# Masks, memory term and token rows as 64-row matmuls in an attention, mixture-of-experts and MLP kernel

## The chip, the cores and the metric

One core of a Trainium2 chip runs the whole program. The metric is the device time of one execution in microseconds (us).

## The reference, cut to what matters

The kernel computes three stages one after another: attention with a memory term, a mixture of experts with one expert per token, and an MLP. The change is in the first, and in the passage from the first to the second.

```python
# attention: B, H, S, D = 4, 8, 576, 64
scores = scale * np.matmul(q, k.transpose(0, 1, 3, 2))
scores = np.where(causal, -1e9, scores)
a = np.exp(scores - scores.max(-1, keepdims=True))
a /= a.sum(-1, keepdims=True) + 1e-09
local = np.matmul(a, v)
q_p = phi(q)
mem_out = einsum('bhsd,bhde->bhse', q_p, M_prev) / (einsum('bhsd,bhd->bhs', q_p, z_prev)[..., None] + 1e-06)
attn = g * mem_out + (1 - g) * local                  # g = sigmoid(beta), per head
# mixture of experts: N, D, E, F = 2304, 512, 8, 1024
logits = x @ w_gate;  e = argmax(logits);  gate_w = softmax(logits)[e]
out = gate_w * (np.maximum(x @ w1[e], 0.0) @ w2[e])
# MLP: 2304 tokens, 512 -> 2048 -> 512, ELU between
```

All is float32 with an accuracy that a single pass of TensorE in reduced precision does not give, so products are made of two halves (hi and lo) in three passes, or as float32 matmuls, which the trace shows as two instructions each.

## The kernel before, in words

**Attention.** A pair is two heads of one batch; there are 16 pairs (4 batches of 4). The 128 partitions hold two heads of 64 dimensions. The 576 query rows are cut into four row tiles of 128 and a short one of 64. For each pair the function `attention` (its inner function `pair`) records these operations:

- q and k are loaded, transposed on TensorE (L549) and split into halves in the table `ab`; phi(q), transposed, is `qpT`.
- Score tiles. For row tiles 0 to 3, `scores` issues six matmuls (L634): three hi and lo combinations for each of two heads, each contracting over that head's 64 partitions, so that the two heads' matmuls use the upper and the lower half of the array. The causal mask follows as a matmul of the bf16 identity with a mask table (L636), one per head, over all 128 rows. The short row tile holds both heads as the rows of one tile, with six 128-row matmuls (L642) and a mask (L643). A score tile takes a two-bank PSUM tile, one bank per head.
- VectorE takes the row minimum (scores carry a negative sign, L651), ScalarE the exponential with its row sum (L656).
- TensorE transposes the weights block by block (L668); ScalarE or VectorE evacuates each block into `aA` (row tiles 0 to 2) or `aB` (3 and 4) (L504, L507).
- The products with v (L771): each head's result goes to 64 of the 128 output partitions.
- The memory term (L739): per row tile one float32 matmul of `qpT` over 128 rows against the table `mb`, which holds one head's columns for the upper 64 rows and the other's for the lower 64, zeros elsewhere, 146 columns. Token rows (L787): likewise `xT`, the product transposed, against the table `iw` (identity and gate weights, 144 columns). Both are made as two blocks of three and two row tiles, in one-bank tiles.
- VectorE scales both (L755 and L792), POOL adds them into the token rows and logits (L803).
- After the last pair of a batch `gate_plan` makes the routing of the batch (L909, L1021 and others).

**PSUM in this stage** is four one-bank tiles (ring `rw`) and two two-bank tiles (ring `rx`, for score tiles and the transposes of q and k).

**What sets the order.** The operations are not run in the order in which they are recorded. Each is handed to a `Plan` with its engine or engines, a cost in ns, what it reads and writes, and a priority: 1000 per pair plus an offset from the table `KNOBS` (`off`). `Plan.order` is a list scheduler: it keeps a time for each engine, takes those operations whose inputs and buffers are there, and among those that could start within a slack it takes the one of lowest priority number. It decides between ScalarE and VectorE too where both are named. `emit` issues the instructions in that order; after that each engine runs in order.

**The passage.** The attention stage and the expert stage are two plans. In the second the first tile's rows of x (table `ex`, gathered in the first) are transposed (L1223), split into halves (L1185 and L1188, in the helper `split`), weights are split part by part in the same helper (eight parts of 1024 columns), and the first expert matmul follows (L1277). The second product of the experts is L1320. The MLP stage is `moe2`.

Of the kernel before, what the change touches and what calls it, by code (L numbers as in the profile page):

```python
# [79 lines left out]
class Op:  # L80
    __slots__ = ("eng", "cost", "fn", "prio", "lat", "need", "users", "slots", "ready", "start", "seq", "why", "dma", "lag", "waits", "dense", "span")


class Plan:
# [10 lines left out]
    def __init__(self, slack=0.0, begin=(), warm=1.0e4, wait=0.0):  # L95
        self.slack, self.begin, self.warm, self.wait = slack, dict(begin), warm, wait
        self.ops, self.wr, self.rd, self.base = [], {}, {}, 0.0

    def op(self, eng, cost, fn, r=(), w=(), prio=0.0, dma=0.0, lag=0.0, dense=1.0, span=(0.0, 1.0e9)):
        o = Op()  # L100
        o.dense, o.span = dense, span
# [33 lines left out]
    def order(self):  # L135
        ready, free, done, queue, work = {}, {}, [], 0.0, {}
# [6 lines left out]
        while len(done) < len(self.ops):  # L143
            best = None
            for e, lst in ready.items():
                cand = []
                for o in lst:
# [17 lines left out]
                    cand.append((t, o.prio, o.seq, o))  # L165
# [21 lines left out]
            if e == "PE":  # L187
# [3 lines left out]
                end = t + o.cost * (1.0 + cold) + (self.wait if o.waits else 0.0)  # L191
# [32 lines left out]
    "m_g": -500, "wq": 0.85, "sa": 60.0, "sm": 50.0, "s2": 0.0, "step": -140.72, "hd": 3300.14,  # L224
    "mem": 23753.60, "xg": 4,
    "wh": [("ACT", "DVE"), ("ACT", "DVE"), ("ACT", "DVE"), ("DVE",), ("ACT",), ("ACT", "DVE"), ("ACT", "DVE"), ("ACT", "DVE")],
    "wl": [("DVE",)] * 8, "ord": [4, 2, 3, 1, 0], "rings": 2, "ab": 2,
    "busy": [0, 0, 0], "early": -20000.00, "late": 500, "mld": -14323.58, "gate": -27170.79,
    "warm": [52, 0.0, 200.0], "qe": ("DVE",),
    "off": {"tk": -12817.78, "tq": -13488.70, "hi": -2210.28, "lo": -31413.21, "px": 6755.77, "phi": -79534.02, "F": -5913.349368048794, "S": 17790.71, "min": 19452.13, "exp": 27411.30, "T": 14069.74, "Te": -6480.68, "fin": 55325.15, "mm": 81816.08, "md": -23369.51, "ms": 75715.68, "av": 48586.94, "ave": 30515.56, "rw": 59524.12, "ls": -7182.97, "add": 6568.91},  # L230
    "wait": 25
# [19 lines left out]
def constants(tc, ctx, c, M_prev, z_prev, beta, w_gate):  # L251
# [12 lines left out]

    c.swap = c.ap.tile([P, P], F32, name="swap")
# [10 lines left out]
    c.iw = c.ap.tile([P, H // 2, 2 * XB], F32, name="iw")  # L276

    MW = XB + 1
    c.mb = c.ap.tile([P, NPAIR, 2 * MW], F32, name="mb")
# [11 lines left out]
    pl.op("POOL", 2600, f, w=["mb", "iw"], prio=400.0)  # L291

    def f():
        for h in range(2):
            nc.sync.dma_start(c.mb[hss[h], :, h * MW:h * MW + D], Mv[h])
        nc.sync.dma_start(wg, w_gate.rearrange("(h d) e -> d h e", d=D))
        nc.sync.dma_start(zr, z_prev.rearrange("b h d -> (b h) d"))
    pl.op("SP", 2600, f, w=["mld"], prio=K["mld"], dma=3000)

    def f():  # L300
        for h in range(2):
            nc.sync.dma_start(c.iw[hss[h], :, h * XB + D:(h + 1) * XB], wv[h])
# [3 lines left out]
    def f():  # L306
        for h in range(2):
            for hp in range(H // 2):
                nc.vector.tensor_copy(c.iw[hss[h], hp, h * XB:h * XB + D], c.ident[hss[h], hss[h]])
# [12 lines left out]
    for h in range(2):  # L322
        for n in range(2):
            def mk(h, n):
                bk = Slot(c.rs)

                def f():
                    for x in range(8):
                        nc.tensor.transpose(bk.t[0:D, x * D:(x + 1) * D], c.mb[hss[h], 8 * n + x, h * MW:h * MW + D], c.ident[hss[h], hss[h]])
                pl.op("PE", 450, f, r=["mld"], w=[bk], prio=K["mem"] - 30)  # L330

                def f():
                    nc.scalar.copy(mT[:, h, 8 * n:8 * n + 8, :].rearrange("p x d -> p (x d)"), bk.t[0:D, :])
                pl.op("ACT", ca(512), f, r=[bk], w=[("mT", h, n)], prio=K["mem"] - 30)
            mk(h, n)
    for h in range(2):
        def mk(h):
# [8 lines left out]
            def f():  # L346
                nc.vector.tensor_copy(c.mb[hss[h], :, h * MW + D:h * MW + XB], bq.t[hss[h], 0:NPAIR * E].rearrange("p (x e) -> p x e", e=E))
                nc.vector.tensor_copy(c.mb[hss[h], :, h * MW + XB:(h + 1) * MW].rearrange("p x o -> p (x o)"),
# [1370 lines left out]
```

## Time and profile before

| what | us |
|---|---|
| three runs | 1000.88, 1000.12, 998.05 |
| their median | 1000.12 |
| the profiled execution | 999.02 |
| its span in the profile | 996.9 |
| TensorE busy | 963.7 |
| TensorE's weight loads | 789.9 |
| VectorE busy | 651.6 |
| ScalarE busy | 453.1 |
| GpSimd (POOL) busy | 140.2 |

The span is what the profiler saw from the first to the last instruction; the execution's own time is 2.1 us more. Weight loads are a row of their own, since they run beside the matmuls. Attention fills the time to about 270 us, the experts to about 592, the MLP the rest.

### The profile page before, as it was taken

How to read it: one execution, taken by the hardware profiler on the slowest of the kernel's cores; microseconds unless marked ns; L12 is line 12 of the kernel's file. 1: busy time of each engine (PE TensorE's matmuls, PEld its weight loads, DVE VectorE, ACT ScalarE, POOL GpSimd, SP SyncE). 2: the span in 40 equal slices, each digit the busy share in tenths (PEclk: the TensorE clock that was granted, in tenths of full speed). 3: DMA queues.
4: the chain of work that ended last, by engine and by line, in shares of the span. 5: the costliest groups of instructions: out<-in, count | busy, mean ns of one | idle time of the engine just before them, and what ended most of it. 6: DMA issues, size and time to landing. Idle time of an engine off the chain costs nothing. (4 is left out here: it accounts for less than half of the span.)

```text
span 996.9 us, 16392 instructions
## 1 busy us (share of the span) xinstructions
PE 963.7 (97%) x5770; PEld 789.9 (79%) x5770; DVE 651.6 (65%) x1307; ACT 453.1 (45%) x945; POOL 140.2 (14%) x260
## 2 busy tenths in 40 slices
PE   9899999999799999999999899899999999999996
PEld 6777877877578888888888688788888888888895
DVE  3878778786786447745798479955565456555553
ACT  3677777775455336634787343322122212212221
POOL 2112211211210011211222111201001000100010
PEclk7999999999999999999999999999999999999998
DMA  6223234235081479349796263111011001100010
GB/s 118 61 66 92 73 70 111 49 97 182 12 299 35 145 244 339 96 158 320 277 361 244 94 212 117 64 32 43 1 42 43 1 1 32 43 1 1 0 43 21
DMA packets 94859, 105.66 MB, mean 106 GB/s; under 512 B 64686, under 2 KB 64686, under 8 KB 92464
## 3 DMA queue, kind: packets, MB, share of 16 engines
q1 hardware_dynamic: 88768, 91.06, 28.8%
q0 software_dynamic: 4800, 13.18, 3.8%
q8 instruction: 46, 0.75, 0.3%
q10 hardware_dynamic: 1200, 0.30, 0.2%
q14 instruction: 45, 0.37, 0.1%
HBM read 85.84 MB, written 21.31 MB: 107 GB/s over the span
## 5 line engine op out<-in xcount | busy, mean ns | idle before, releaser
L1538 ACT ACTIVATE elu<-pt 128x512 f32<-128x512 f32 x72 | 43.1, 598 | 251.1 <-PE pt L1530 250.9
L1563 PE MATMUL pt<-w,gh 128*128 128x512 f32 x432 | 134.7, 393 | 1.7 <-DVE gh L1429 1.7
L1320 PE MATMUL pm<-w,hh 128*128 128x512 f32 x368 | 127.1, 407 | 2.9 <-ACT y L1333 2.9
L1277 PE MATMUL pm<-w,xh 128*128 128x512 f32 x368 | 119.9, 395 | 2.0 <-DVE xh L1185 2.0
L1546 DVE TENSOR_SCALAR elu<-elu 128x512 f32<-128x512 f32 x72 | 30.6, 426 | 117.3 <-ACT elu L1538 117.3
L656 ACT ACTIVATE a<-pat,st 128x128 f32<-128x128 f32 (+2 forms) x144 | 78.7, 554 | 34.7 <-DVE st L651 34.3
L1563 PEld LDWEIGHTS pt<-w,gh 128*128 128x128 f32 x432 | 79.5, 188 | 18.4 <-DVE gh L1429 2.3
L1563 PE MATMUL pt<-w,gl 128*128 128x512 f32 x216 | 84.9, 393 | 3.0 <-POOL gl L1435 3.0
L1320 PEld LDWEIGHTS pm<-w,hh 128*128 128x128 f32 x368 | 69.9, 190 | 18.5 <-ACT y L1333 3.4
L1277 PEld LDWEIGHTS pm<-w,xh 128*128 128x128 f32 x368 | 69.9, 190 | 17.4 <-POOL y L1177 2.2
L651 DVE TENSOR_REDUCE st<-pat 128x2 f32<-128x256 f32 (+4 forms) x80 | 64.5, 809 | 27.2 <-PE pat L636 19.5
L1277 PE MATMUL pm<-w,xl 128*128 128x512 f32 x184 | 72.8, 396 | 1.2 <-DVE xl L1188 1.2
L1320 PE MATMUL pm<-w,hl 128*128 128x512 f32 x184 | 73.6, 400 | 0.0
L1530 PE MATMUL pt<-yTh,w 128*128 128x256 f32 (+1 forms) x288 | 68.6, 318 | 0.0
L803 POOL TENSOR_TENSOR raw<-ms,ls 128x24 f32<-128x24 f32 (+3 forms) x120 | 41.6, 380 | 179.0 <-DVE ls L792 138.3
L668 PE MATMUL pa<-ident,a 128*128 128x128 f32 x400 | 59.7, 277 | 2.7 <-ACT a L656 1.4
L1550 DVE SCALAR_TENSOR_TENSOR tnh<-tnh,elu 128x512 f32<-128x512 f32 x72 | 49.6, 690 | 6.2 <-ACT tnh L1542 0.5
L1258 DVE TENSOR_TENSOR w<-wraw,w 128x1024 fp32r<-128x1024 f32 x40 | 47.2, 1222 | 8.3 <-ACT w L1253 6.4
L668 PEld LDWEIGHTS pa<-ident,a 128*128 128x128 f32 x400 | 45.3, 142 | 8.7 <-ACT a L656 6.1
L1530 PEld LDWEIGHTS pt<-yTh,w 128*128 128x128 f32 x288 | 48.6, 189 | 4.5
L1188 DVE TENSOR_TENSOR hl<-pm,hh 128x512 fp32r<-128x512 f32 x46 | 31.5, 685 | 31.2 <-ACTq L1251 16.2
L1554 DVE SCALAR_TENSOR_TENSOR tnh<-pt,tnh 128x512 f32<-128x512 f32 x72 | 49.7, 690 | 2.9
(319 smaller groups left out, 2053.3 us busy)
## 6 DMA issues: line engine op xcount, KB each, us to landing
wraw<-in_moe_w_dram SPq DMA_DIRECT2D x24, 1024.0 KB, 7.2
wrbw<-in_moe_w_dram SPq DMA_DIRECT2D x12, 1024.0 KB, 7.4
wide<-in_moe_w_in_dram SPq DMA_DIRECT2D x16, 512.0 KB, 6.0
wide<-in_moe_w_out_dram SPq DMA_DIRECT2D x16, 512.0 KB, 4.3
wf<-half SPq DMA_DIRECT2D x24, 256.0 KB, 3.7
q<-in_q_dram SPq DMA_DIRECT2D x32, 128.0 KB, 2.6
v<-in_v_dram SPq DMA_DIRECT2D x32, 128.0 KB, 2.6
half<-wf SPq DMA_DIRECT2D x8, 512.0 KB, 4.3
```

The source lines that it names most:

```text
L651: nc.vector.tensor_reduce(ss.t[:, 2 * i:2 * i + (2 if i < 4 else 1)], src(), axis=AX.X if i < 4 else AX.XY, op=ALU.min)
L656: nc.scalar.activation(sa[i].t[:, h, :] if i < 4 else sa[4].t[:, 0:S].rearrange("p (y n) -> p y n", y=2), src()[:, h, :] if i < 4 else src ...
L668: nc.tensor.transpose(w.t[:, y * P:(y + 1) * P], t[:, j * P:(j + 1) * P], c.ident)
L803: e.tensor_tensor(o, a, b, op=ALU.add)
L1258: nc.vector.tensor_sub(wlo[2 * k + q], src(q), whi[2 * k + q].bitcast(F32))
L1277: nc.tensor.matmul(g[hf].t, a.t[:, cc, :], b[:, 512 * hf:512 * (hf + 1)], start=(cc == 0 and n == 0), stop=(cc == 3 and n == 2))
L1320: nc.tensor.matmul(y.t, a.t[:, 2 * (q % 2) + jj, :], b[:, 512 * jj:512 * (jj + 1)], start=(q == 0 and jj == 0 and n == 0), stop=(q == 3 an ...
L1530: nc.tensor.matmul(h.t[:, n * j + n0:n * j + n1], w(cc, a, ft), b(cc), start=(cc == 0 and x == 0), stop=(cc == 3 and x == 2))
L1538: nc.scalar.activation(se.t, h.t, AF.Exp)
L1550: nc.vector.scalar_tensor_tensor(st.t, st.t, 0.0, se.t, op0=ALU.min, op1=ALU.mult)
L1554: nc.vector.scalar_tensor_tensor(st.t, h.t, 0.0, st.t, op0=ALU.max, op1=ALU.add)
L1563: nc.tensor.matmul(acc[a].t, y.t[:, n * j + P * a:n * j + P * (a + 1)], wsub(1, k, ft // 2)[:, ft % 2, :], start=(ft == 0 and x == 0), sto ...
```

## The change

Four things change in the attention stage, one in the passage, one in the planner.

1. *Masks.* Instead of one 128-row matmul per head there are two 64-row matmuls per head, for the upper and the lower half of the mask's rows, with the tables `id64` and `mask64` (L657).
2. *Memory term and token rows.* Instead of five 128-row matmuls against padded tables there are ten 64-row matmuls, one per row tile and head, each head into a bank of its own (L767 and L812). The tables lose their padding, and POOL no longer clears it.
3. *PSUM* becomes four two-bank tiles, one ring for everything. Each memory block is one tile instead of two, and VectorE scales it in one instruction; `a`, `xT` and `ls` get second buffers where they had one.
4. *Weights.* The transposes of one row tile for both heads go into one tile and are evacuated by one copy.
5. *Passage.* The new function `first_parts` makes tile 0's transposes of x (L1186), both halves of x and the halves of the first weight part inside the attention plan. The second plan leaves them out.
6. *Planner.* An operation on TensorE has a tiling (`mode`: 0 for 128 rows, 1 for 64 rows, 2 for the products into 64 partitions). A change of tiling costs 90 ns in the plan, and an operation of the present tiling is preferred by `stick`. The offsets in `KNOBS` are all new, and so are the order of the row tiles and a few costs.

```diff
+    DRAIN = 90.0
...
-                    cand.append((t, o.prio, o.seq, o))
+                    cand.append((t, o.prio - (self.stick if e == "PE" and o.mode == mode else 0.0), o.seq, o))
...
-                end = t + o.cost * (1.0 + cold) + (self.wait if o.waits else 0.0)
+                end = t + o.cost * (1.0 + cold) + (self.wait if o.waits else 0.0) + (self.DRAIN if o.mode != mode else 0.0)
+                mode = o.mode
...
-    "wl": [("DVE",)] * 8, "ord": [4, 2, 3, 1, 0], "rings": 2, "ab": 2,
+    "wl": [("DVE",)] * 8, "ord": [3, 4, 2, 1, 0], "rings": 4, "ab": 2, "nq": 2, "nv": 2, "na": 2, "na4": 2, "nx": 2, "nls": 2, "wide": 1, "de": ("DVE", "POOL"),
...
-    "wait": 25
+    "wait": 25, "first": 44674.95, "stick": 239909.83
...
+        nc.vector.tensor_copy(c.mask64[:, 0:D], c.mask4)
+        for h in range(2):
+            nc.vector.tensor_copy(c.id64[h * D:(h + 1) * D, D:P], c.identb[h * D:(h + 1) * D, h * D:(h + 1) * D])
...
-            nc.gpsimd.memset(c.mb[hss[h], :, (1 - h) * MW:(2 - h) * MW], 0.0)
-            nc.gpsimd.memset(c.iw[hss[h], :, (1 - h) * XB:(2 - h) * XB], 0.0)
...
-                for h in range(2):
-                    nc.tensor.matmul(s.t[:, 512 * h + i * P:512 * h + n], c.identb, c.maskb, start=False, stop=True)
+                for y in range(2):
+                    for h in range(2):
+                        hs = slice(h * D, (h + 1) * D)
+                        nc.tensor.matmul(s.t[:, 512 * h + i * P + y * D:512 * h + n], c.id64[hs, (1 - y) * D:(1 - y) * D + P], c.mask64[hs, 0:P - y * D],
+                                         start=False, stop=(y == 1))
...
-                    for i in range(ni):
-                        nc.tensor.matmul(w.t[:, i * 2 * MW:(i + 1) * 2 * MW], sqT.t[:, (i0 + i) * P:(i0 + i + 1) * P], c.mb[:, p, :],
-                                         start=True, stop=True)
+            for i in range(NI):
+                for h in range(2):
+                    hs = slice(h * D, (h + 1) * D)
+                    nc.tensor.matmul(wm.t[:, 512 * h + i * MW:512 * h + (i + 1) * MW], sqT.t[hs, i * P:(i + 1) * P], c.mb[hs, p, :], start=True, stop=True)
...
-                        nc.tensor.matmul(w.t[:, i * 2 * XB:(i + 1) * 2 * XB], sx.t[:, (i0 + i) * P:(i0 + i + 1) * P], c.iw[:, hp, :],
-                                         start=True, stop=True)
+                        for h in range(2):
+                            hs = slice(h * D, (h + 1) * D)
+                            nc.tensor.matmul(w.t[:, 512 * h + i * XB:512 * h + (i + 1) * XB], sx.t[hs, (i0 + i) * P:(i0 + i + 1) * P], c.iw[hs, hp, :], start=True, stop=True)
...
+def first_parts(c):
+
+    nc, pl, K = c.nc, c.pl, c.K
+    wx, pr = Slot(c.rx), K["first"]
+
+    def f():
+        for cc in range(4):
+            nc.tensor.transpose(wx.t[:, cc * P:(cc + 1) * P], c.ex[:, cc:DM:4], c.ident)
+    pl.op("PE", 436, f, r=[c.se], w=[wx], prio=pr)
+    xh, xl = [t.rearrange("p c n -> p (c n)") for t in c.x0]
+    split(c, lambda: wx.t[:, 0:512], lambda: xh, lambda: xl, 512, [wx], "x0h", "x0l", pr, True, ("ACT", "DVE"), ("DVE",))
+    for q in range(len(c.wq)):
+        hi, lo = c.wq[q]
+        split(c, lambda q=q: c.wraw[0][0][:, 1024 * q:1024 * (q + 1)], lambda hi=hi: hi, lambda lo=lo: lo, 1024, [("raw", 0, 0)], ("hi", q), ("lo", q),
+              pr + 10.0 * q, False, ("ACT", "DVE"), ("DVE",))
```

How the order on TensorE moves is shown at two places. In these rows a name before the arrow is the output (`pa` a one-bank PSUM tile, `pat` a two-bank one), after it stand what is loaded and streamed; x6 is a run of six alike. A float32 matmul counts once here.

The first place is a settled pair. Before, TensorE's order around two score tiles:

```order
L636 MATMUL pat_89<-maskb,identb 128x128
L771 MATMUL pa_86<-aB_217,v_194 64x192 x2
L771 MATMUL pa_84<-aA_215,v_194 64x384 x2
L771 MATMUL pa_84<-aA_215,v_194 64x256 x2
L771 MATMUL pa_84<-aA_215,v_194 64x128 x2
L771 MATMUL pa_86<-aB_217,v_194 64x192 x2
L668 MATMUL pa_85<-ident,a_200 128x128 x2
L634 MATMUL pat_89<-ab_196 128x256 x6
L636 LDWEIGHTS identb
L636 MATMUL pat_89<-maskb,identb 128x128
L636 LDWEIGHTS identb
L636 MATMUL pat_89<-maskb,identb 128x128
```

The order now, from token rows of the pair before to the memory term of this one (L812, L653, L657, L767):

```order
L812 MATMUL pat_92<-iw,xT_233 128x72 x10
L653 MATMUL pat_93<-ab_199 128x512 x6
L657 LDWEIGHTS id_111
L657 MATMUL pat_93<-mask_110,id_111 128x128
L657 LDWEIGHTS id_111
L657 MATMUL pat_93<-mask_110,id_111 128x128
L657 LDWEIGHTS id_111
L657 MATMUL pat_93<-mask_110,id_111 128x64
L657 LDWEIGHTS id_111
L657 MATMUL pat_93<-mask_110,id_111 128x64
L767 MATMUL pat_91<-mb,qpT_227 128x73 x10
```

and right behind it, from the first transposes of the weights (L691) to the first product with v (L794):

```order
L691 MATMUL pat_92<-ident,a_207 128x128 x2
L691 MATMUL pat_94<-ident,a_209 128x128 x4
L664 MATMUL pat_92<-ab_199 128x288 x6
L665 LDWEIGHTS identb
L665 MATMUL pat_92<-mask_107,identb 128x64
L691 MATMUL pat_94<-ident,a_211 128x128 x6
L560 MATMUL pat_93<-ident,k_195 128x128 x5
L691 MATMUL pat_91<-ident,a_213 128x128 x8
L560 MATMUL pat_94<-ident,q_193 128x128 x5
L691 MATMUL pat_92<-ident,a_215 128x128 x5
L736 MATMUL pat_93<-st_219,swap 128x1
L794 MATMUL pat_91<-aA_223,v_203 64x384 x2
```

Before, products of one pair with v (L771) and transposes of the weights (L668) stand between the score tiles of the next pair, and each mask is a 128-row matmul. Now the 64-row work of a pair stands in one run: its four score tiles, their masks, the pair before's token rows and its own memory term. Behind it come the transposes, with the short row tile (L664) and the transposes of k and q (L560) among them, and then all products with v. The short row tile's scores (`pat_92`) take the tile of the first transposes, and the last transposes (from `a_215`) are those of the short row tile.

The second place is the end of the stage. Before, on TensorE:

```order
L711 MATMUL pa_84<-st_212,swap 128x1
L771 MATMUL pa_85<-aB_217,v_194 64x192 x8
L771 MATMUL pa_85<-aB_217,v_194 64x64 x2
L787 MATMUL pa_86<-iw,xT_222 128x144 x3
L787 MATMUL pa_87<-iw,xT_222 128x144 x2
L1223 MATMUL pm_3277<-ident,ex 128x128 x4
L1133 UNCONDITIONAL_BRANCH
L1277 MATMUL pm_3273<-w_3306,xh_3308 128x512
```

The order now:

```order
L1186 MATMUL pat_94<-ident,ex 128x128 x4
L691 MATMUL pat_92<-ident,a_214 128x128 x8
L691 MATMUL pat_93<-ident,a_217 128x128 x5
L736 MATMUL pat_91<-st_221,swap 128x1
L794 MATMUL pat_94<-aA_224,v_205 64x384 x2
L794 MATMUL pat_94<-aA_224,v_205 64x256 x2
L794 MATMUL pat_94<-aA_224,v_205 64x128 x2
L794 MATMUL pat_92<-aB_226,v_205 64x192 x8
L794 MATMUL pat_92<-aB_226,v_205 64x64 x2
L812 MATMUL pat_93<-iw,xT_233 128x72 x6
L812 MATMUL pat_91<-iw,xT_233 128x72 x4
L1329 MATMUL pm_3360<-wq_82,x_80 128x512
```

The transposes of x for the first expert tile (L1223 before, L1186 now) stood behind the last token rows; now they stand among the last pair's transposes, and the first expert matmul (L1277 before, L1329 now) is the next instruction behind the token rows (L812). Its weights are the part `wq` that the attention plan has split.

## Rows read from the trace of the kernel before

**Rows 1.** Page, first lines: span, and busy time, share and instructions by engine.
```profile
span 996.9 us, 16392 instructions
...
PE 963.7 (97%) x5770; PEld 789.9 (79%) x5770; DVE 651.6 (65%) x1307; ACT 453.1 (45%) x945; POOL 140.2 (14%) x260
```
**Rows 2.** Windows: us, busy by engine (x instructions), PEclk, DMA share, GB/s.
```profile
48.00:62.20 14.20, 14.20 (x122) 10.42 (x120) 10.45 (x26) 9.52 (x28) 1.70 (x5) 1.00 0.28 64
90.10:107.30 17.20, 17.20 (x166) 14.03 (x165) 16.07 (x60) 12.98 (x40) 4.60 (x14) 1.00 0.44 123
122.10:182.10 60.00, 59.62 (x541) 47.52 (x540) 47.76 (x136) 45.58 (x131) 11.00 (x33) 1.00 0.33 80
242.50:261.90 19.40, 16.58 (x139) 12.87 (x137) 13.13 (x38) 8.89 (x27) 7.13 (x17) 1.00 0.07 18
261.90:273.40 11.50, 8.54 (x69) 6.32 (x66) 6.22 (x20) 4.88 (x12) 0.65 (x3) 1.00 0.01 2
273.40:290.00 16.60, 14.88 (x65) 12.13 (x65) 15.40 (x27) 8.60 (x13) 4.88 (x5) 0.90 0.71 263
```
**Rows 3.** Line L642's instructions: min/median/max ns, first and last start.
```profile
L642 PEld LDWEIGHTS pat<-ab x96: 187/188/192, 31.2 to 262.5; 128*128 128x128 f32 x96
```
**Rows 4.** TensorE's timeline, two stretches from 113 and 119.9: start, duration, instruction.
```profile
113.02 0.62 PE L634 MATMUL pat<-ab 64*128 64x256 f32 x6
113.58 0.29 PE L636 MATMUL pat<-maskb,identb 128*128 128x128 bf16 x2
...
119.95 0.60 PE L668 MATMUL pa<-ident,a 128*128 128x128 f32 x4
120.48 0.79 PE L634 MATMUL pat<-ab 64*128 64x384 f32 x6
121.21 0.29 PE L636 MATMUL pat<-maskb,identb 128*128 128x128 bf16 x2
121.33 1.04 PE L668 MATMUL pa<-ident,a 128*128 128x128 f32 x8
```
**Rows 5.** TensorE's weight loads (PEld): timeline, then two lines' instructions.
```profile
118.62 1.28 PEld L787 LDWEIGHTS pa<-iw,xT 128*128 128x128 f32 x10
119.83 0.48 PEld L668 LDWEIGHTS pa<-ident,a 128*128 128x128 f32 x4
120.48 0.47 PEld L634 LDWEIGHTS pat<-ab 64*128 64x128 f32 x6 [0.17 <-issue]
...
226.90 0.52 PEld L1021 LDWEIGHTS pa<-r_sel,r_tab 72*128 72x128 f32 x4 [0.87 <-DVE r_tab L916]
...
L634 PEld LDWEIGHTS pat<-ab x384: 182/185/335, 17.8 to 259.3; 64*128 64x128 f32 x192
L787 PEld LDWEIGHTS pa<-iw,xT x160: 186/190/204, 41.9 to 269.5; 128*128 128x128 f32 x160
```
**Rows 6.** Groups by shape, 40 to 235: busy us, mean ns | idle before them.
```profile
L651 DVE TENSOR_REDUCE st<-pat 128x2 f32<-128x1024 f32 x13 | 15.9, 1223 | 4.2 <-PE pat L636 4.2
L651 DVE TENSOR_REDUCE st<-pat 128x1 f32<-128x576 f32 x13 | 9.8, 756 | 7.0 <-PE pat L643 7.0
L656 ACT ACTIVATE a<-pat,st 128x576 f32<-128x576 f32 x13 | 9.7, 745 | 1.4 <-DVE st L651 1.4
```
**Rows 7.** Timeline, the end of the attention stage and the first expert tile.
```profile
268.44 1.49 PE L787 MATMUL pa<-iw,xT 128*128 128x144 f32 x10
273.45 0.47 PE L1277 MATMUL pm<-w,xh 128*128 128x512 f32 x1 [2.02 <-DVE xh L1185]
281.74 0.40 PE L1277 MATMUL pm<-w,xh 128*128 128x512 f32 x1
...
272.01 0.69 DVE L1185 CAST w<-wraw 128x1024 fp32r<-128x1024 f32 x1
272.62 0.68 DVE L1185 CAST xh<-pm 128x512 fp32r<-128x512 f32 x1
273.22 1.22 DVE L1188 TENSOR_TENSOR w<-wraw,w 128x1024 fp32r<-128x1024 f32 x1
```

More of the change, by code (lines that the diff above doesn't have):

```diff
@@ L80 @@
 class Op:
-    __slots__ = ("eng", "cost", "fn", "prio", "lat", "need", "users", "slots", "ready", "start", "seq", "why", "dma", "lag", "waits", "dense", "span")
+    __slots__ = ("eng", "cost", "fn", "prio", "lat", "need", "users", "slots", "ready", "start", "seq", "why", "dma", "lag", "waits", "dense", "span", "mode")
 class Plan:
@@ L135, in order @@
     def order(self):
-        ready, free, done, queue, work = {}, {}, [], 0.0, {}
+        ready, free, done, queue, work, mode = {}, {}, [], 0.0, {}, 0
         for o in self.ops:
@@ L771, in f @@
                                 nc.tensor.matmul(x.t[h * D:(h + 1) * D, o:n], svi.t[:, j, h, :], mv, start=(j == 0), stop=(j == tiles[-1]))
-                        pl.op("PE", (n - o) / 0.6 + 40, f, r=[svi] + [(so, i, h, y) for i, h, y in blocks if i in tiles and (y == j)], w=[x], prio=at("av") + g)
+                        pl.op("PE", (n - o) / 0.6 + 5, f, r=[svi] + [(so, i, h, y) for i, h, y in blocks if i in tiles and (y == j)], w=[x, (sx, "own", g, j)], prio=at("av") + g, mode=2)
                     mm(j)
@@ L1150, in gather, with f, split, ha @@
     c.pl.op("POOL", 1040, f, dma=734, **kw)
+def first_parts(c):
+    nc, pl, K = c.nc, c.pl, c.K
+    wx, pr = Slot(c.rx), K["first"]
+    def f():
+        for cc in range(4):
[7 more added lines that the diff above has]
+              pr + 10.0 * q, False, ("ACT", "DVE"), ("DVE",))
+def split(c, src, hi, lo, n, rd, wh, wl, pr, psum, eh, el):
+    nc, pl = c.nc, c.pl
+    def ha():
+        nc.scalar.copy(hi(), src())
+    def hv():
+        nc.vector.tensor_copy(hi(), src())
+    def lv():
+        nc.vector.tensor_sub(lo(), src(), hi().bitcast(F32))
+    def lp():
+        nc.gpsimd.tensor_sub(lo(), src(), hi().bitcast(F32))
+    he = {"ACT": (ca(n, sb=not psum), ha), "DVE": (cv(n) if psum else cv2(n), hv)}
+    le = {"DVE": (cv(n), lv), "POOL": (cpt(n), lp)}
+    for es, d, r, w in ((eh, he, rd, wh), (el, le, rd + [wh], wl)):
+        pl.op(es, [d[x][0] for x in es], [d[x][1] for x in es], r=r, w=[w], prio=pr)
 def moe(tc, c, w1, w2, tiles):
@@ L1378, in moe @@
         pl.op("SP", 480, f, r=[("tile", K["wp"]), "y0"], w=[sr], prio=1.0e6, dma=1456)
-        split(src, lambda: c.w0.t[:, 0], lambda: c.w0.t[:, 1], 1024, [sr], "w0h", "w0", 1.0e6, False, ("ACT", "DVE"), ("DVE", "POOL"))
+        split(c, src, lambda: c.w0.t[:, 0], lambda: c.w0.t[:, 1], 1024, [sr], "w0h", "w0", 1.0e6, False, ("ACT", "DVE"), ("DVE", "POOL"))
 def moe2(tc, c, w_in, w_out, out):
```

218 lines of the change are left out of this document (114 added, 104 removed).

## The prediction

> **What bounds the kernel now.** I read the page first, then the windows by stage, then TensorE's timeline in a settled stretch, then the weight loads. By the page [rows 1] TensorE (PE) is busy for 97% of 996.9 us, so nothing off PE is worth much unless PE waits for it. The profiled execution took 999.0 us, 1.1 below the median of the three runs shown (1000.1); I make the sum against 999.0 and shift it at the end.
>
> The windows [rows 2] are cut mostly where the score block of the last, short row tile (L642) starts, once per pair of heads, 16 times from 31.2 to 262.5 [rows 3]. The reader is to see that from 48 on PE has hardly a hole: a clean pair takes 14.2 us, one in which a batch's gate is computed 17.2, four pairs together 60.0 with PE busy for 59.6. VectorE (DVE) has 10.45 us of work in the clean pair and 16.07 in the gate pair. Only the edges have holes: the last two windows of the stage (19.4 - 16.6 = 2.8 us idle and 11.5 - 8.5 = 3.0), and the first expert tile, where the mean granted clock is 0.90, so that some of it ran at 1.2 GHz.
>
> A busy PE is not yet a PE that streams. In the timeline [rows 4] four transposes start at 119.95 and a score block at 120.48: 0.53 us, where four at their own pace take 4 x 0.11 = 0.44 (the pace from their loads, (0.48 - 0.14) / 3 [rows 5]). So about 0.09 us goes by when the array is retiled from 128 rows to 64. The block of 256 columns takes 0.56 us to its mask (113.02 to 113.58), that of 384 columns 0.73: 128 columns more, three times, are 0.17, so 128 columns stream in 0.057, and of the 0.73 only 0.51 is streaming. The other 0.22 are the first weight load in the open (0.11) and the drain for the 128-row mask (0.11). **A change of tiling costs 0.10 to 0.20 us**; an entry into the score tiling the most, the exit into the bf16 mask the least. I take 0.16, nearer to the entry, since behind the values' products too the next load lies in the open.
>
> **The change, part by part.**
> *Changes of tiling.* Before, masks, memory term and token rows are 128-row matmuls, so every score tile goes into the 64-row tiling and out of it. Counted by shape in PE's order up to the first expert matmul, the tiling changes 216 times before and 62 times now: in a settled pair into the score tiles (with token rows and memory term among them), out to the transposes, and into the values' 64-column products. 154 x 0.16 = **-24.6 us**; bounds -15 and -31.
>
> *Memory term and token rows.* Each was ten full-height instructions (five matmuls in two passes) at 0.12, (1.28 - 0.19) / 9 [rows 5]. Each has twenty now, in ten side-by-side pairs of 73 or 72 columns, half the streaming. But the weights still have 128 columns, and a load gets no shorter with fewer rows: 185 ns with 64 rows, 190 with 128 [rows 5]. Where next to nothing streams (L1021, four columns), loads alone set the pace: (0.52 - 0.19) / 3 = 0.11. The two heads' loads run side by side (six in 0.47; one by one they would need 5 x 0.11 + 0.19). So a block goes from 1.2 to 10 x 0.11 = 1.1; bounds 0.6 (streaming alone) and 1.2. 32 blocks x 0.12 = **-3.8 us**. The Trainium skill, "TensorEngine Tiling (Array Packing)", section Theoretical Speedup, promises up to twofold for a contraction of at most 64 rows, by which the sum would have 32 x 0.6 = 19 us here. Against it stands the Trainium skill, "TensorE: Matmul & The Clock Gate", section LDWEIGHTS: a load takes as long as its columns say, whatever the rows; rows 5 agree, with 185 and 190 ns.
>
> *Masks.* Before, from mask to next transpose it is 0.12 (121.21 to 121.33) [rows 4]. Now two pairs stream 128 and 64 columns (0.06 + 0.03), and behind them lies the next tile's load of 0.11, of which the short pair hides 0.03: 0.17. It could be nothing more or 0.1 more; I take 0.04 for 64 tiles: **+2.6 us**.
>
> *What PE then waits for.* A clean pair falls by 10 x 0.16 + 0.24 - 0.16 = 1.7 to 12.5 us, a gate pair to 15.5. DVE's 16.07 us in a gate pair hardly shrink (it reads each memory block once in place of twice, but takes more of the copies), and its first reduction starts only after the first score tile, 0.5 into the pair: 16.5. **+3 us** for three gate pairs. In a clean pair DVE's 10.45 us fit. The chain does not quite: with four tiles for all, the short tile's scores take the bank of the first transposes, whose copy must end first, and the last transposes wait for that tile's reduction and exponential (0.76 and 0.75), queued behind the widest reduction (1.22) [rows 6]. Walked through with these durations it leaves about 0.35 of waiting per pair: **+4.5 us** for thirteen pairs; bounds 0 and 1.2 per pair.
>
> *The end of the stage.* Before, the last token rows start at 268.44 and the first expert matmul at 273.45 [rows 7], behind a transpose, two casts and a subtraction. Now the transposes (L1186), both halves of x and the first weight part are made inside the last pairs, and the expert matmul stands right behind the token rows in PE's order: 5.0 less 1.3 for the rows themselves is 3.7; the transposes take 0.4 of that, and DVE has 0.68 + 0.68 + 0.69 + 1.22 of splitting ahead of its last copies, some of which shows: **-3.0 us**; bounds 0 and -5. Late next is the second weight part: DVE needs 0.69 + 1.22 = 1.9 for one [rows 7], now after its last sums, and the first product, which still ended at 282.1, waits for part after part. With one part of them ready I take half of its 1.9, **-1.0 us**; bounds 0 and -1.9.
>
> *At nothing:* the loads of q, k, v and weights, whose order on SP's queue stays nearly the same, two pairs ahead of use (uncovered, a late load would cost PE its length); the clearing of the padded tables on POOL that falls away, long done when the first score tile starts at 17.8 [rows 5]; the expert and last stages, whose instructions keep their kinds and counts.
>
> Sum: -24.6 - 3.8 + 2.6 + 3.0 + 4.5 - 3.0 - 1.0 = -22.3. 999.0 - 22.3 = 976.7, and 1.1 for the median: **978 us**. With the bounds of the tiling's price and of the wait: 967 to 989.
>
> **The rivals.**
> *Loads hidden (0.10).* If 64-row loads run further ahead than rows 5 show, each block is 0.6: 32 x 0.5 = -16, of which DVE and the exponentials eat half: 970, and 958 with the high price of a tiling change. For it: the heads' loads run side by side. Against: L1021.
> *Four tiles are too few (0.20).* PE stops for PSUM. Before, two two-bank tiles serve the scores and four banks the rest; now one transposed block of 128 columns holds as much as a score tile. A wait of 1.2 per pair in place of 0.35 is +11 to +13: 990, up to 995. For: the token rows' tile is freed by a DVE read that queues behind three reductions. Against: before, PE is full with two tiles for the scores, and now they draw on four.
> *One pair at a time, slower (0.10).* Before, the values' products of one pair stand between the score tiles of the next and cover a late exponential. Now a pair's scores, transposes and products stand in a row, with ten transposes of q and k as the only cover. If the last transposes have to wait through the reduction, the exponential and the steps between engines (0.15 from DVE's end at 273.30 to PE's matmul at 273.45 [rows 7], three of them), it is 0.76 + 0.75 + 0.4, and another 0.4 for the bank: 2.3 per pair, 35 us over fifteen pairs: 999.0 - 26.8 + 35 + 1.1 = 1008. It decides from 26.8 / 15 = 1.8 us per pair; around 1.8 it is no change (0.03).
>
> **How the numbers follow.** The forecast has 0.57. From 958 to 995 lie the forecast, most of the case of loads and most of that of four tiles: 0.83. A measurement of this kernel can tell about 0.3%, 3 us, from no change. Faster by more: 0.57 + 0.10 + 0.19 = 0.86; the same 0.04; slower 0.10.
>
> **What would show it.** Right: clean pairs of 12.5 to 13.3 us between starts of the short tile's scores, gate pairs above 16; the ten load pairs of a memory block 0.11 apart; three drains per pair; the first expert matmul near 251 in place of 273.45, right behind the token rows; the stages behind it as long as before. Wrong: pairs as long as before, with PE idle until ACT's exponentials or DVE's reductions (the third rival); memory blocks of 0.6 (the first); an expert stage that grows by what the first stage gives.

## The result and the profile after

The changed kernel takes 972.4 us (median of four runs, 970.84 to 973.37) against 999.1 of the kernel before on the same chip: a ratio of 0.9731, 95% interval 0.9708 to 0.9755, or 26.7 us less. Predicted were 978 us with a range of 958 to 995, so the time lies inside; 22.3 us less were forecast. The total is close, but several of its terms were not, and the later sections say which.

The page of the changed kernel, first lines; they answer to [rows 1]:

```profile
span 970.8 us, 17051 instructions
...
PE 941.2 (97%) x6218; PEld 785.3 (81%) x6218; DVE 656.4 (68%) x1223; ACT 431.3 (44%) x885; POOL 123.4 (13%) x185
```

TensorE has 448 matmul records more than before and is busy for 22.5 us less; that is most of the 26.1 us that the span fell. VectorE, with 84 instructions fewer, is busy for 5 us more. The records count the time of a change of tiling as busy, so a lower busy time with more matmuls is no contradiction (the four pairs with 128-row masks, below, show it: they are 3.70 us longer, all of it busy).

Windows of the changed kernel, with the columns of [rows 2]: a gate pair, a clean pair, four pairs together, the last two windows of the stage, and the first expert tile.

```profile
79.18:95.59 16.41, 15.24 (x182) 12.84 (x182) 15.35 (x52) 11.00 (x34) 2.07 (x4) 1.00 0.46 130
95.59:108.79 13.20, 13.17 (x156) 11.46 (x157) 11.10 (x21) 9.68 (x28) 1.93 (x4) 1.00 0.31 68
108.79:164.93 56.14, 54.81 (x650) 47.28 (x650) 49.32 (x115) 40.04 (x115) 7.97 (x13) 1.00 0.35 86
217.00:243.10 26.10, 25.68 (x303) 21.71 (x303) 21.36 (x41) 16.53 (x49) 5.24 (x7) 1.00 0.09 23
243.10:245.00 1.90, 1.27 (x21) 1.13 (x21) 1.03 (x4) 0.32 (x1) 0.00 (x0) 1.00 0.00 0
245.00:264.00 19.00, 17.37 (x80) 12.90 (x81) 15.10 (x31) 10.49 (x16) 6.07 (x7) 1.00 0.78 279
```

Four pairs take 56.1 us in place of 60.0, a clean pair 13.2. In the gate pair TensorE now stands idle for 1.2 us (16.41 - 15.24) while VectorE has 15.35 us of work. The first expert matmul starts at 245.00 in place of 273.45 [rows 7], 28.4 us earlier; the expert stage then takes 2.5 us longer than before (300.9 us from its first matmul to the end of its last, against 298.4) and the last stage as long as before, which makes the 26.1 us of the span.

TensorE's timeline of the changed kernel in a settled pair, up to the short row tile (columns as in [rows 4]):

```profile
102.84 0.63 PE L653 MATMUL pat<-ab 64*128 64x256 f32 x6
103.31 0.26 PE L657 MATMUL pat<-mask,id 64*128 64x128 bf16 x4
103.41 0.60 PE L653 MATMUL pat<-ab 64*128 64x256 f32 x6
103.85 0.26 PE L657 MATMUL pat<-mask,id 64*128 64x128 bf16 x4
103.94 0.77 PE L653 MATMUL pat<-ab 64*128 64x384 f32 x6
104.55 0.26 PE L657 MATMUL pat<-mask,id 64*128 64x128 bf16 x4
104.65 1.31 PE L812 MATMUL pat<-iw,xT 64*128 64x72 f32 x20
105.76 0.94 PE L653 MATMUL pat<-ab 64*128 64x512 f32 x6
106.55 0.26 PE L657 MATMUL pat<-mask,id 64*128 64x128 bf16 x4
106.64 1.31 PE L767 MATMUL pat<-mb,qpT 64*128 64x73 f32 x20
107.89 0.87 PE L691 MATMUL pat<-ident,a 128*128 128x128 f32 x6
```

From one score tile of 256 columns to the next it is 0.53 us (103.41 to 103.94), mask included; before, such a block took 0.56 to its mask alone. The mask costs 0.09 (103.85 to 103.94). The token rows take 1.11 (104.65 to 105.76). Only the last step, from the memory term to the transposes at 107.89, leaves the tiling, and with 1.25 it is 0.14 longer than the token rows.

### The profile page after: what moved, and what is told of

It reads as the page before. It is cut to its first block, busy times and chain, and to the rows that moved or that the text cites. A ratio compares the mean times of both kernels' runs of the same rounds, so it can differ in the third digit from the quotient of the medians.

```text
span 970.8 us, 17051 instructions
## 1 busy us (share of the span) xinstructions
PE 941.2 (97%) x6218; PEld 785.3 (81%) x6218; DVE 656.4 (68%) x1223; ACT 431.3 (44%) x885; POOL 123.4 (13%) x185
## 5 line engine op out<-in xcount | busy, mean ns | idle before, releaser
L678 ACT ACTIVATE a<-pat,st 128x128 f32<-128x128 f32 (+2 forms) x144 | 78.1, 551 | 24.7 <-DVE st L673 24.1
L691 PE MATMUL pat<-ident,a 128*128 128x128 f32 x400 | 55.2, 277 | 1.7 <-DVE ms L779 1.4
L1329 PE MATMUL pm<-w,x 128*128 128x512 f32 x216 | 52.0, 392 | 1.2 <-DVE w L1206 0.9
L1615 PEld LDWEIGHTS pt<-w,gl 128*128 128x128 f32 x216 | 40.9, 189 | 13.3 <-POOL gl L1487 3.7
L828 POOL TENSOR_TENSOR raw<-ms,ls 128x80 f32<-128x80 f32 (+2 forms) x45 | 30.0, 694 | 168.7 <-DVE ls L816 168.7
L1484 DVE TENSOR_TENSOR gl<-tnh,gh 128x512 fp32r<-128x512 f32 x67 | 46.3, 690 | 4.1
L1329 PEld LDWEIGHTS pm<-w,x 128*128 128x128 f32 x216 | 40.2, 188 | 10.4 <-DVE w L1206 1.4
L653 PE MATMUL pat<-ab 64*128 64x256 f32 (+2 forms) x384 | 47.1, 359 | 0.3
```

The costliest lines, as they stand in the source:

```text
L653: nc.tensor.matmul(s.t[:, 512 * h:512 * h + m], row(y)[hs, i * P:(i + 1) * P], row(x)[hs, 0:m], start=(k == 0), stop=False)
L678: nc.scalar.activation(sa[i].t[:, h, :] if i < 4 else sa[4].t[:, 0:S].rearrange("p (y n) -> p y n", y=2), src()[:, h, :] if i < 4 else src ...
L691: nc.tensor.transpose(w.t[:, y:y + P], t[:, j * P:(j + 1) * P], c.ident)
L1329: nc.tensor.matmul(g[hf].t, a.t[:, cc, :], b[:, 512 * hf:512 * (hf + 1)], start=(cc == 0 and n == 0), stop=(cc == 3 and n == 2))
L1484: nc.vector.tensor_sub(lo(), src(), hi().bitcast(F32))
L1615: nc.tensor.matmul(acc[a].t, y.t[:, n * j + P * a:n * j + P * (a + 1)], wsub(1, k, ft // 2)[:, ft % 2, :], start=(ft == 0 and x == 0), sto ...
```

## The experiments

The time of an experiment is compared with the 972.4 of the changed kernel or the 999 of the kernel before. Where it matters in which stage the time went, stretches of the traces are compared.

**128-row masks in the new order.** All else, order included, stays; only the masks leave the tiling and come back to it.

```diff
-                for y in range(2):
-                    for h in range(2):
-                        hs = slice(h * D, (h + 1) * D)
-                        nc.tensor.matmul(s.t[:, 512 * h + i * P + y * D:512 * h + n], c.id64[hs, ...], c.mask64[hs, ...], start=False, stop=(y == 1))
+                for h in range(2):
+                    nc.tensor.matmul(s.t[:, 512 * h + i * P:512 * h + n], c.identb, c.maskb, start=False, stop=True)
```

> The changed kernel with the masks of row tiles 0 to 3 as one 128-row matmul per head again; the order of everything else on TensorE is kept, so that 124 changes of tiling are added (55 to 179 in the attention stage). By the prediction's price of 0.16 us a change it takes 124 x 0.16 = 20 us more, 992. By the price that the changed kernel's trace suggests, 0.10 us (0.77 us off a clean pair that has some ten changes fewer, with 0.3 of waiting and 0.24 of shorter blocks in it), 12 to 13 us more, 985. If changes of tiling are hidden and the gain comes from the start, the passage and the order alone, within 2 us of 972.

Measured: 987.66 us, 15.3 more. The same stretch of TensorE's timeline in this kernel, one pair further on:

```profile
110.75 0.61 PE L653 MATMUL pat<-ab 64*128 64x256 f32 x6
111.30 0.28 PE L655 MATMUL pat<-maskb,identb 128*128 128x128 bf16 x2
111.51 0.62 PE L653 MATMUL pat<-ab 64*128 64x256 f32 x6
112.07 0.28 PE L655 MATMUL pat<-maskb,identb 128*128 128x128 bf16 x2
112.28 0.80 PE L653 MATMUL pat<-ab 64*128 64x384 f32 x6
```

From tile to tile it is 0.77 us in place of 0.53: 0.24 for two changes of tiling, though two instructions fewer run. Four pairs, first with these masks, then of the changed kernel:

```profile
51.10:110.80 59.70, 58.47 (x619) 47.83 (x619) 49.81 (x114) 40.54 (x114) 7.97 (x12) 1.00 0.33 81
```

```profile
46.90:102.90 56.00, 54.76 (x653) 47.24 (x651) 49.16 (x115) 40.05 (x114) 7.98 (x12) 1.00 0.35 87
```

3.70 us more for 32 changes is **0.116 us a change**; the 15.3 us of the whole kernel, for 124 changes, are 0.123. The 128-row masks alone bring the four pairs nearly back to the 60.0 that they took before the change. The Trainium skill, "TensorEngine Tiling (Array Packing)", section Key Properties, states that a change of tiling drains TensorE, and gives no price; this run agrees and gives one.

**64-row masks in the old order.** The same part, added to the kernel before and nothing else.

> The kernel before with 64-row masks and nothing else; its order is kept, in which transposes or products with v stand behind most masks, so that changes of tiling fall from 210 to 160 only. By 0.115 us a change 50 x 0.115 = 6 us less than before, 994. By 0.16, 8 us less, 992. If the 64-row masks themselves gave the gain that the masks' run took away (15 us), 985. If changes of tiling count for nothing, within 2 us of 999.6.

Measured: 993.42 us, ratio 0.9947 (0.9927 to 0.9966), 5.3 us less (3.4 to 7.3 by the interval), where 50 changes at 0.116 give 5.8. The same instructions are worth 15 us in the one order and 5 in the other: a 64-row mask saves what the changes around it save, and nothing more that these runs show.

**A planner that knows nothing of tilings.**

```diff
-    DRAIN = 90.0
+    DRAIN = 0.0
...
-    "wait": 25, "first": 44674.95, "stick": 239909.83
+    "wait": 25, "first": 44674.95, "stick": 0.0
```

> The changed kernel with a planner that knows nothing of tilings (no cost of a change, no preference for the present one); all instructions stay. Its order has 152 changes of tiling in the attention stage in place of 55. With 0.115 us a change, as the masks' run gave it (3.7 us for 32 changes in four pairs), 97 x 0.115 = 11 us more, 983. By 0.16, 988. If the planner's knowledge matters little, within 2 us of 972. If the order also brings PSUM waits, beyond 990.

Measured: 1005.25 us, 32.9 more than the changed kernel and slower than the kernel before (1.0058, 1.0037 to 1.0079). All the new instructions are there. 97 changes at 0.116 are 11 us. From the first score tile to the first expert matmul TensorE is idle for 24.1 of 259.6 us, in the changed kernel for 7.0 of 227.7, so 17 us more are waiting. The view of TensorE's waits (46 to 274; us in all, times, longest) names most of it:

```profile
PE pat L794 <- DVE aB L518: 8.0, 6, 1.4
PE pat L794 <- ACT aB L515: 3.5, 7, 1.0
PE pat L691 <- ACT a L678: 3.0, 13, 0.3
```

In that order products with v stand right behind the transposes and wait for the copies of `aB`, 11.5 us in all. The run's limit: the offsets were fitted with tilings in the plan; a plan without them but with offsets of its own wasn't tried.

**Four two-bank tiles in the kernel before.** `"rings": 4`, and the one-bank ring falls back on the two-bank one.

> The kernel before with four two-bank PSUM tiles for everything and nothing else changed; its planner with its old offsets then finds an order with 144 changes of tiling in place of 210. If PSUM kept the first pair slow, its last product ends some 5 us earlier than the 41.7 of before, and with 66 changes at 0.10 the time falls by 10 or so, to 988. If the first pair is slow for its order and its 128-row masks and blocks, its end stays within 2 us of 41.7, and the time lies between 990 and 1003, since the offsets belong to other tiles.

Measured: 1061.87 us, ratio 1.0625 (1.0598 to 1.0651), worse than either theory had it. The pairs run two by two: their last products with v end at 49.8 and 52.5, then at 87.5 and 90.3, and between them TensorE waits (40 to 336, same view):

```profile
PE pat L668 <- ACT a L656: 8.9, 15, 1.4
PE pat L549 <- ACT a L656: 6.5, 6, 2.3
PE pat L739 <- DVE qpT L603: 5.4, 4, 1.4
```

The transposes of q and k (L549) read nothing that the exponential (L656) makes, so their 6.5 us are waits for a tile that it still reads. The rival of the prediction that four tiles are too few thus fits the old offsets; with the new ones such waits are few. With four tiles the first pair ends at 49.8 in place of 41.7. The tiles alone do not make it faster, but since the planner's order changed with them, what PSUM adds to its length isn't told.

**Token rows as 128-row matmuls** in the same places of the new order, against a padded table (the memory term's padded table no longer fits beside the new buffers, so that half wasn't tried). VectorE scales each block in two instructions again.

> The changed kernel with the token rows as five 128-row matmuls of 144 columns against a padded table again, in the same place of the same order: 16 blocks, 15 of them between two score tiles, so 30 changes of tiling more. By 0.16 us a change and 0.12 a block: 4.8 + 1.9 = 6.7 us more, 979. By 0.10 a change: 5 us more, 977. If the halves side by side streamed at twice the pace (0.6 a block off), 13 to 15 more. If neither counts, within 1.5 us of 972.

Measured: 976.73 us, 4.3 more; the first expert matmul starts 5.8 us later than in the changed kernel (250.76). The order has 29 changes more (two around each of fifteen blocks, one less behind the last), which are 3.4 of the 5.8 and leave 2.4 for sixteen blocks, **0.15 us a block**; forecast was 0.12. The later stages, which this run did not touch, give some of the 5.8 back, so the stage and not the total is read here. The weight loads of the changed kernel show why it isn't more:

```profile
104.62 1.20 PEld L812 LDWEIGHTS pat<-iw,xT 64*128 64x128 f32 x20
106.62 1.20 PEld L767 LDWEIGHTS pat<-mb,qpT 64*128 64x128 f32 x20
```

Twenty loads in ten side-by-side pairs take 1.20 us, (1.20 - 0.19) / 9 = 0.11 from pair to pair: halving the rows shortens no load.

**Without first_parts.** The transposes and halves of x and the first weight part go back into the expert plan; the rest of the attention order stays.

> The changed kernel without first_parts: the transposes of x, its halves and the first weight part are made in the expert plan again; the rest of the attention order is the same. By the prediction 3.0 for the end of the stage and 1.0 for the weight part: 4 us more, 976. If the passage also keeps the granted clock up in the first expert tile (1.8 us lost at half clock in the kernel before, none in the changed one), 5 to 6 more. If VectorE's splitting sets the first tile's end either way, 0 to 2 more.

Measured: 973.56 us (five runs, 972.83 to 974.48), 1.2 more, which is hardly beyond the noise. TensorE's timeline of this run:

```profile
242.71 1.34 PE L812 MATMUL pat<-iw,xT 64*128 64x72 f32 x20
244.68 0.74 PE L1269 MATMUL pm<-ident,ex 128*128 128x128 f32 x4 [0.63 <-DVE ls L816]
247.27 0.76 PE L1325 MATMUL pm<-w,x 128*128 128x512 f32 x1 [1.85 <-DVE x L1203]
248.91 7.66 PE L1325 MATMUL pm<-w,x 128*128 128x512 f32 x23 [0.88 <-DVE x L1206]
```

and of the changed kernel, first TensorE, then VectorE:

```profile
245.00 1.66 PE L1329 MATMUL pm<-wq,x 128*128 128x512 f32 x6 [0.63 <-DVE ls L816]
246.96 0.70 PE L1329 MATMUL pm<-w,x 128*128 128x512 f32 x2 [0.29 <-DVE w L1203]
248.59 3.92 PE L1329 MATMUL pm<-w,x 128*128 128x512 f32 x16 [0.94 <-DVE w L1206]
...
247.33 6.89 DVE L1206 TENSOR_TENSOR w<-wraw,w 128x1024 fp32r<-128x1024 f32 x6
```

On the spot the passage is worth 2.3 us (247.27 against 245.00), and at the end of the expert stage 0.7 of that is left (546.52 against 545.85). With the first part ready TensorE starts earlier and then waits for the next parts, which VectorE still splits, six subtractions back to back. That does not explain the loss. The last long wait of the expert stage, here and in the changed kernel, ends 1.9 us apart (539.11 and 537.22):

```profile
539.11 0.50 PE L1368 MATMUL pm<-w,hh 128*128 128x512 f32 x1 [2.93 <-ACT y L1381]
```

```profile
537.22 0.80 PE L1372 MATMUL pm<-w,hh 128*128 128x512 f32 x1 [2.93 <-ACT y L1385]
```

So 1.9 of the 2.3 us reach this place. Another 1.2 us go behind it, where the granted clock falls: over the last 16 us of the stage it has a mean of 0.89 in this run and 0.79 in the changed kernel. The expectation's question about the clock has an answer too: without first_parts it falls in the first expert tile, with a mean of 0.89 from 245 to 275 us, some 6.6 us at 1.2 GHz, where the changed kernel keeps 1.00. The 5 to 6 us that the expectation named for that case did not come.

**Splitting on POOL too.** `"wl": [("DVE", "POOL")] * 8`, which moves two of those subtractions.

> The changed kernel whose planner may give the low halves of the first expert tile's weights to POOL as well as to VectorE; it gives two of seven to POOL. If VectorE's splitting sets the first tile's pace (six subtractions of 1.15 back to back from 247.33, with TensorE waiting 0.29 and 0.94 for them), 1 to 2 us less, 971. If the tile's pace is set by something else, or the waits come later, within 1 us of 972. If POOL's subtraction is slower than the planner thinks, up to 2 us more.

Measured: 972.64 us, no difference. The first tile's second product starts 0.2 us earlier, that of the next tile 1.2 later, and by the stage's end it evens out. What sets the time from there on is not these subtractions alone.

**The two kernels once more, unchanged,** for the start of the program.

> The changed kernel once more, unchanged, to see how long the half-clock stretch at the start lasts: 6.8 us in its first profile, 13.7 in that of the kernel before and in that of the masks' run, whose set-up is the changed kernel's. If the length belongs to the kernel, 6.8 again; if it varies from execution to execution, any of 6.8, 10.2 and 13.7 may come, and up to 3.4 us of the difference of two profiles is not the change's. Time within 2 us of 972 either way.

> The kernel before once more, unchanged. If the half-clock stretch belongs to the kernel, 13.7 us of it again from about 12.1; if it varies, 6.8 or 10.2 may come, with a first pair that ends up to 3.4 us earlier than 41.7. Time within 2 us of 999.

Measured: 974.13 and 998.56 us. The windows from 12 to 26 us, of before, before again, the changed kernel and the changed kernel again; the third column from the right is the granted clock:

```profile
12.00:26.00 14.00, 13.86 (x81) 11.36 (x80) 6.26 (x23) 4.62 (x16) 0.00 (x0) 0.51 0.40 85
```

```profile
12.00:26.00 14.00, 12.68 (x93) 9.57 (x92) 7.85 (x30) 6.92 (x20) 0.00 (x0) 0.76 0.49 107
```

```profile
12.00:26.00 14.00, 13.85 (x128) 10.95 (x129) 8.50 (x27) 7.39 (x24) 0.00 (x0) 0.76 0.40 86
```

```profile
12.00:26.00 14.00, 13.97 (x115) 10.85 (x113) 7.18 (x22) 6.64 (x22) 0.00 (x0) 0.64 0.41 87
```

At a mean of 0.51 some 13.7 of the 14 us ran at 1.2 GHz, at 0.76 some 6.8. The same kernel shows both, so the length of the stretch is not the change's doing. In the two profiles that are compared here it was 13.7 before and 6.8 after, and half of the difference, 3.4 us, belongs to the start and not to the change. The Trainium skill, "TensorE: Matmul & The Clock Gate", Part 1, says that the slow stretch at a kernel's start varies from run to run of one kernel; these windows agree that it varies, though the page speaks of the first matmuls and here the clock falls after 12 to 14 us.

**Dense matmuls in the set-up,** eight of 512 columns between those of 8 columns, behind which the clock had fallen.

> The changed kernel with eight 512-column bf16 matmuls, whose results nobody reads, between the 64x8 matmuls of the set-up. In the changed kernel the granted clock falls to 1.2 GHz at 14.4 us, behind these small matmuls, and rises at 21.0. If it falls because TensorE streams little there, it stays at 2.4 and the first pair gives back 3.3 us less about 0.9 for the extra matmuls: 970. If it falls all the same, within 1 us of 973.

Measured: 977.73 us (four runs, 976.07 to 978.87), 5.3 more. Neither theory held: the clock fell at 12.7 and stayed at 1.2 GHz for 13.7 us, and the first score tile started at 22.63 in place of 17.32. Since that stretch varies by itself, one profile doesn't tell why; that more streaming keeps the clock up at this place isn't shown.

**Measured prices in the planner:** 116 in place of 90 for a change, 1110 and 222 in place of 700 and 140 for the blocks.

> The changed kernel with the planner's prices set to what the traces measured: 116 ns for a change of tiling (90), 1110 ns for a memory block (700), 222 ns per row tile of token rows (140). The order on TensorE stays almost the same, with 55 changes of tiling. If the order alone matters, within 2 us of 972. If the wrong prices make TensorE wait for buffers, 2 to 4 less; if the offsets were fitted to the wrong prices, 2 to 5 more.

Measured: 974.98 us (971.19 to 976.74), 2.6 more, which these runs hardly tell from no change. In its trace the pairs of the first batch take 14.0 us, against 13.2 to 13.7. So the planner's wrong prices cost nothing that these runs show; that its offsets were fitted to them is likely and not shown. No run gave a version clearly faster than the changed kernel.

## Why the prediction was right, and where it was not

The stage up to the first expert matmul is best compared between two profiles with the same slow stretch of 6.8 us: 253.2 us from the first score tile in the second profile of the kernel before (17.53 to 270.69), 227.7 in the changed kernel (17.32 to 245.00): 25.5 us less. The forecast for this stage was 21.3 less.

*The price of a change of tiling* was taken too high. "I take 0.16, nearer to the entry" was the step: the four pairs give 0.116, the two whole kernels 0.123 (15.3 us for 124 changes) and 0.106 (5.3 for 50), near the lower end. So 154 changes are 17.9 us and not 24.6. The 0.16 lies between an exit at 0.11 and an entry at 0.20 (0.09 ahead of the score block [rows 4] and 0.11 of a load in the open). But from one score tile to the next without a change it still is 0.53 us, of which by the prediction's own pace 0.34 stream and 0.09 are the mask: the 0.10 that is left is nearly as long as that load, so the load seems to stay in the open; no run separates it. The mechanism, that changes of tiling cost TensorE time which it shows as busy, held. The 2.6 us for the new masks, in which the prediction charged the next tile's load, had no place of their own: 0.116 already holds the masks' own columns and what follows them. Both terms together were forecast at 22.0 and are 17.9, 4.1 less.

*Memory term and token rows* were forecast at 0.12 a block, and the token rows gave 0.15, at load pairs 0.11 apart as forecast. The rival of hidden loads (0.6 a block) fell, and with it the twofold pace of the Trainium skill, "TensorEngine Tiling (Array Packing)", section Theoretical Speedup: no run here shows it; the ten load pairs, 0.11 apart, are as long as the token rows' 1.11.

*Gate pairs* were forecast to fall to 16.5 and fell to 16.4, with VectorE busy for 15.35 of it and TensorE idle for 1.2. Of that, in the pair shown, 0.60 us are a wait for VectorE (`ms`, L779) and 0.34 one for ScalarE's copy (`aA`, L515). That VectorE alone sets this end isn't shown; no run relieved it.

*The wait in a clean pair* was forecast at 0.35 us, at the short row tile's scores, which take the tile of the first transposes. All weight loads of that line (L664) in the changed kernel, and what was waited for ahead of them (us, times):

```profile
L664 PEld LDWEIGHTS pat<-ab x96: 186/188/192, 24.0 to 236.6; 128*128 128x128 f32 x96
...
  ACT aA L515: 3.1, 12
  DVE aA L518: 0.5, 2
```

3.1 / 12 = 0.26 us a pair, at that place and for that copy. It is the weight loads that stand idle there; the matmul records hide it, with TensorE busy for 13.17 of the clean pair's 13.20 us. TensorE loses the time all the same: the six transposes ahead of the short row tile take 0.90 us (107.89 to 108.79), the six behind it 0.69 (96.53 to 97.22 in the pair before). The waiting for the reduction and the exponential that was feared behind it shows in no clean pair as a wait of TensorE. With the lower price of a change and this wait the clean pair lands at 13.2, inside the 12.5 to 13.3 that were named as the sign of a right forecast.

*The holes at the edges* were seen and not priced. [rows 2] shows 2.8 and 3.0 us of idle TensorE at the end of the stage. The prediction took 3.0 back for the passage and left the rest. In the second line below, the last 28.2 us before the last token rows have 3.06 us of idle time in the kernel before; in the changed kernel the last 26.1 us have 0.42. How that comes about wasn't tried in a run of its own. The first pair is a second such place: its last product with v ended at 41.7, or 38.9 in the second profile of the kernel before, and now ends at 32.9. The first line is the stretch from the first score tile to that product in the second profile of the kernel before, the third is the same stretch now:

```profile
17.53:38.90 21.37, 18.27 (x154) 14.08 (x153) 17.54 (x62) 13.52 (x40) 0.55 (x3) 0.96 0.37 84
```

```profile
240.30:268.50 28.20, 25.14 (x210) 19.61 (x208) 17.55 (x49) 14.05 (x40) 7.13 (x17) 1.00 0.09 21
```

```profile
17.32:32.90 15.58, 14.76 (x144) 12.34 (x143) 11.97 (x33) 11.11 (x30) 0.56 (x3) 0.88 0.42 93
```

The idle time fell from 3.1 to 0.8 us. The rest of the 5.8 us is no gain of this kind: before, two score tiles, a memory block and transposes of the next pair stood in that stretch, and now they come behind it. The changed order issues all four score tiles of the first pair ahead of its memory term, where the old one stretched them over 12 us; that this is the cause is argued from the order, not shown.

*The passage* was forecast at 3.0 and 1.0 us. On the spot it gave 2.3, at the last wait of the expert stage 1.9, and 0.7 to 1.2 at the end. So of the step "with one part of them ready I take half of its 1.9" nothing came that lasts: the first product ends 4.1 us earlier than without first_parts (248.59 + 3.92 = 252.5 against 248.91 + 7.66 = 256.6), but the stage keeps no more of it than those 1.9. Which later wait takes the rest isn't shown.

*The expert stage* was to be "as long as before" but for that, and took 2.5 us longer. Half of this lies ahead of its last long wait, 2.93 us for ScalarE's `y`, which in the kernel before ended here:

```profile
564.41 0.50 PE L1320 MATMUL pm<-w,hh 128*128 128x512 f32 x1 [2.93 <-ACT y L1333]
```

That is 291.0 us behind the first expert matmul (273.45); in the changed kernel it is 292.2 (245.00 to 537.22), without first_parts 291.8 (247.27 to 539.11). So 0.4 of the 1.3 us are the passage, and 0.9 come without it and stay open. The other 1.2 us lie behind that wait. These windows hold the last 16 us, of the kernel before and of the changed one:

```profile
556.00:572.00 16.00, 12.88 (x51) 9.73 (x48) 7.33 (x7) 6.74 (x9) 1.46 (x2) 0.89 0.03 12
```

```profile
530.00:546.00 16.00, 12.93 (x43) 9.61 (x41) 6.94 (x7) 6.11 (x8) 1.48 (x2) 0.79 0.07 25
```

In both TensorE waits for 2.9 us and then runs at 1.2 GHz, 3.4 us before and 6.8 in the changed kernel. Both profiles of the changed kernel show it. But the runs with 128-row masks and with 128-row token rows, whose expert stage is the changed kernel's, have 0.89 there, so the change isn't shown to be the cause. At the start of the stage the reverse holds: the 3.4 us at 1.2 GHz behind the old passage (mean clock 0.90 [rows 2]) are gone.

By terms: 17.9 for tilings, 4.8 for 32 blocks at 0.15 (the memory term's taken as the token rows'), 2.3 for the passage, less 3 x 1.2 = 3.6 for the gate pairs and 3.1 + 0.5 = 3.6 for the waits, make 17.8 of the 25.5 us. The holes closed at both edges, 3.06 - 0.42 = 2.6 at the end and 3.1 - 0.8 = 2.3 in the first pair, make it 22.7. The other 2.8 us stay unassigned. The whole stage shows where they are, in the second profile of the kernel before and in the changed kernel:

```profile
17.53:270.69 253.16, 242.21 (x2136) 190.70 (x2135) 195.36 (x558) 176.41 (x503) 44.04 (x127) 1.00 0.31 82
```

```profile
17.32:245.00 227.68, 220.66 (x2583) 189.51 (x2583) 195.70 (x462) 158.74 (x451) 31.75 (x49) 0.99 0.35 92
```

TensorE is busy for 21.6 us less and idle for 3.9 less. The idle terms (passage, edges, gate pairs) make 3.6 of the 3.9. Tilings and blocks, less the waits that show as busy, make 19.1 of the 21.6, so nearly all that is unassigned lies in busy time.

So the stage came out near its forecast partly by luck: tilings and masks were forecast 4.1 us too high, and against that stand 4.9 us of closed holes that no term held and the 2.8 that no run assigns. Of the 26.1 us between the two profiles that the result compares, 25.5 are this stage, 2.9 the start with its shorter stretch at 1.2 GHz, and the expert stage took 2.5 back.

Two bounds of the prediction do not follow from its terms. Its 967 takes the low ends of both the tiling's price and the wait, its 989 only the high end of the wait; both high ends give 999. And the first rival's 958 lies some 6 us below what its own terms make, 970 - 6.4.

## What to carry to other kernels

Count the changes of TensorE's tiling in its order and price them by a run that adds some without moving anything else; here one costs 0.11 to 0.12 us, is shown as busy time, and 154 fewer are worth more than all shorter blocks. A cheaper instruction is worth only what the order makes of it: the same 64-row masks gave 5 us in the old order and 15 in the new one, and all the new instructions with a planner that ignores tilings were slower than the kernel before. What work taken ahead of a stage gains is read at several places behind it: of 2.3 us at the start of the expert stage 1.9 were left at its last wait, and 0.7 at its end, where a longer stretch at 1.2 GHz and not the work itself took the difference.

## What the runs showed of the hardware that was not expected

The stretch at 1.2 GHz early in the program was 6.8, 10.2 or 13.7 us long in the thirteen profiles at hand, and each of the two kernels that were profiled twice shows two of these lengths. It is worth up to 3.4 us here, as much as several of the terms above, so profiles should be compared from a point behind it, or between profiles with the same stretch. At the end of the expert stage one and the same wait of 2.9 us was followed by none, 3.4 or 6.8 us at 1.2 GHz (a mean of 1.00, 0.89 or 0.79 over the last 16 us), and runs with the same expert stage show 0.89 and 0.79. What was forecast and holds at the new matmuls: two float32 weight loads of 64 rows run side by side without slowing each other (ten pairs in 1.20 us), and a 64-row load is no shorter than one of 128 rows.
